# Threshold attention and a squared-ReLU layer on one core: the second visit's turns moved ahead of the first masks, the last chunk's stores given to SyncE's queue

## The chip, the core and the metric

The kernel runs on one core of one Trainium2 chip. The metric is the device time of one execution in microseconds (us). A core has five engines, each working through its own list of instructions in order: TensorE (PE in the profile, with its weight loads as PEld), VectorE (DVE), ScalarE (ACT), GpSimd (POOL) and SyncE (SP), which only issues DMAs and waits. Semaphores order the engines among each other. DMAs are issued here by SyncE's queue, by GpSimd's queue and, at the very start, by ScalarE's.

## The reference

There are 8 batches of 8 heads, each with 576 rows of 64 values. Of each row of scores only those within tau of the maximum keep their weight. The result goes through a two-layer network with a squared ReLU.

```
scores = 0.125 * q @ k^T                                # (8, 8, 576, 576)
scores = where(scores >= max(scores) - tau, scores, -1e9)
attn = exp(scores - max(scores));  attn /= sum(attn) + 1e-9
x = (attn @ v), heads side by side                       # (4608, 512)
out = relu(x @ w_in)**2 @ w_out                          # w_in (512, 2048), w_out (2048, 512)
```

All inputs and the output are float32.

## The kernel before, in words

**Attention.** Heads are taken in pairs, and the work on a pair is cut into visits. The first eight visits split the four head pairs of the first batch in two: visits 0 to 3 take the first two blocks of 128 query rows of each pair, visits 4 to 7 the rest. A visit is a list of steps, one per block of 128 query rows; the first steps are (visit 0, block 0), (visit 0, block 1), (visit 1, block 0), and so on. The rows of a visit's queries and keys lie in `rows_in`, in two sets used alternately; the set for visit 1 lies in a spare part of the tile `wo`, so the profile names it `wo`. Both have to be turned before they can be used: `prep(n)` (L211) calls `prep_part` twice, and each call is one transpose on VectorE (L226), first into `qT`, of which there is one, then into one of two `kT`. The rows themselves were loaded by `load_qk` (L160), whose DMAs are L168 and L171.

**A step** goes through these parts, with the two heads of the pair as two halves of each tile:

- `scores` (L237): matmuls of `qT` with `kT` into the PSUM tiles `s` (L246), and the maxima of each row on VectorE (L268). The tiles of step 1 are called `second`; all others use the same two tiles `s`, so the scores of step 2 must wait for the masks of step 0.
- `exponents` (L278): bias and threshold, then exp, on ScalarE (L281, L282, L284).
- `threshold` (L287): the masks on VectorE (L296), which read scores and exponents, and the sums' reciprocals (L298, L299).
- `divide` (L301): GpSimd scales the weights (L304, L306).
- two steps later `turn` (L321): TensorE turns the weights (L330), ScalarE copies them to `wT` (L331); and `mix` (L429): the products with `v` (L432), which ScalarE copies to `xT`.

**The network.** Once 256 tokens are ready, a chunk of it is queued as pieces (`mlp_in` L473, `product` L540, `pair_in` L635, `mlp_out` L512), and `fill` (L769) puts pieces between the parts of the steps, by the planner's rate. There are 18 chunks (`NCH`). The last two are done together in their first layer. The second layer of a chunk is seven products (L555); what is added up of them in `osb` goes out in two halves of 128 tokens with `store_rows` (L532, the DMA is L534), the second half first. For the last chunk, these are the last things that the program does: a sum on VectorE (L582), a store, one more product, a sum (L585), a store.

**The weights.** They come as 32 pieces by SyncE (L125), and are rounded piece by piece through ScalarE (L138, L139), VectorE (L141, L143) and GpSimd (L145, L147), the first of them at step 2.

**What sets the order.** The schedule is written by hand: what the main loop over steps (L851) emits first comes first on each engine, and the waits follow from which tiles an instruction reads and writes. At the start, ahead of the loop, stand the loads of visits 0 and 1, the values of visit 0, three weight pieces, `prep(0)`, and twenty transposes that only keep TensorE busy (L276). In step 0 the loop emits `scores(0)`, `exponents`, then `scores(1)` at once (L908), then `threshold` and the division. In step 1, which is the last of visit 0, it emits `exponents`, then `prep(1)` (L890, by the flag `lay`), then `threshold`. So VectorE has the order: maxima of steps 0 and 1, masks of step 0, turns for visit 1, masks of step 1, maxima of step 2.

**The end of the program** is line L975: SyncE waits for what is still on its way, every engine drains, and GpSimd collects the others before all end.

Of the kernel before, what the change touches and what calls it, by code (L numbers as in the profile page):

```python
# [19 lines left out]
def kernel(  # L20
# [10 lines left out]
    nc = tc.nc  # L31
# [3 lines left out]
    P = 128  # L35
# [8 lines left out]
    NCH = n_tokens // TCH  # L44
# [52 lines left out]
    osb = const.tile([P, 2, d_model], FP32, name="osb")  # L97
# [62 lines left out]
    def load_qk(n):  # L160


        for x, t in ((rows_of(n)[1], k), (rows_of(n)[0], q)):
            for m in range(4):
                src, to = rows_32(t, n, m), x[m * 32:(m + 1) * 32, :, :]
                queue = nc.scalar if n == 0 and m % 2 else nc.sync
                last = REST // 32 if t is k and m >= 2 and not by_dma(n) else 0
                queue.dma_start(out=to[:, last:, :], in_=src[:, 0:S // 32 - last, :])  # L168
                if last:
                    queue = nc.gpsimd if n == 0 else nc.sync  # L170
                    queue.dma_start(out=to[:, 0:last, :], in_=src[:, S // 32 - last:, :])  # L171
# [39 lines left out]
    def prep(n):  # L211

        prep_part(q, n)
        prep_part(k, n)

    def split_left(n):

        if NBLK in visits[n][1] and not paired(n):
            for u in range(2):
                rows = slice(u * D, (u + 1) * D)  # L220
                nc.scalar.copy(qmid[rows, u * D:(u + 1) * D], qT[rows, NBLK * P:S])

    def prep_part(t, n):
        to, rows = (qT, rows_of(n)[0]) if t is q else (kT[n % 2], rows_of(n)[1])
        arrived(rows)
        nc.vector.transpose(to, rows.rearrange("p c d -> p (c d)"))  # L226
# [10 lines left out]
    def scores(s):  # L237


        vis, i = steps[s]  # L240
        n = 2 if i < NBLK or paired(vis) else 1
        sc = [second[u] if s == 1 else psum.tile([P, 2, 512], FP32, tag=f"s{u}", name=f"s{u}")
              for u in range(n)]

        def term(u, half, rows, lhsT, keys, to=slice(0, P)):
            nc.tensor.matmul(sc[u][to, half, 0:HALF], lhsT, keys[rows, half * HALF:(half + 1) * HALF],  # L246
                             start=True, stop=True)

        if i == NBLK and paired(vis):
            for half in range(2):  # L250
                for v_ in range(2):
                    for u in range(2):
                        rows, cols = slice(u * D, (u + 1) * D), slice(v_ * D, (v_ + 1) * D)
                        term(u, half, rows, qmid[rows, cols], kT[v_], cols)
        elif i == NBLK:
            for half in range(2):
                term(0, half, slice(0, P), qmid, kT[vis % 2])
        else:
            halves = [(half, u) for half in range(2) for u in range(n)]
            if early():  # L260
                halves.sort(key=lambda x: x[1])
            for half, u in halves:
                rows = slice(u * D, (u + 1) * D)
                term(u, half, rows, qT[rows, i * P:(i + 1) * P], kT[vis % 2])
        st = stats[s % len(stats)]
        mx = st[:, 0, 0:n]
        for u in range(n):
            nc.vector.tensor_reduce(out=mx[:, u:u + 1], in_=sc[u][:, :, 0:HALF], axis=AX.XY, op=ALU.max)  # L268

        w = w_slots[(s - first_dma) % (2 if by_dma(vis) else 3)][:, 0:n, :]  # L270
        weights[vis, i] = w, sc, st
# [6 lines left out]
    def exponents(vis, i):  # L278
        w, sc, st = weights[vis, i]
        mx, thr, bias = (st[:, j, 0:len(sc)] for j in range(3))  # L280
        nc.scalar.activation(out=bias, in_=mx, func=AF.Copy, scale=-SCALE)  # L281
        nc.scalar.activation(out=thr, in_=mx, func=AF.Identity, bias=ntau8)  # L282
        for u in range(len(sc)):
            nc.scalar.activation(out=w[:, u, :].rearrange("p (h k) -> p h k", h=2), in_=sc[u][:, :, 0:HALF],  # L284
                                 func=AF.Exp, bias=bias[:, u:u + 1], scale=SCALE)
# [245 lines left out]

    def store_rows(j, t0, t1):  # L532
        lo = j * TCH
        nc.gpsimd.dma_start(out=out[lo + t0 * P:lo + t1 * P, :].rearrange("(t p) d -> p t d", p=P), in_=osb[:, t0:t1, :])  # L534

# [144 lines left out]
    def paired(n):  # L682

        return n >= 3 * HP
# [8 lines left out]
    def by_dma(n):  # L693

        return n >= 3 * HP - 1
# [21 lines left out]
    chunk_at, j = {}, 0  # L717
# [9 lines left out]
    def early():  # L727
        return state["step"] < min(chunk_at)
# [12 lines left out]
    def add_chunk(j):  # L741
        waiting.extend(pieces_of(j))
# [59 lines left out]
    for s, (n, i) in enumerate(steps):  # L802
# [3 lines left out]
        more = nxt < len(visits)  # L806
# [16 lines left out]
        if more:  # L823
            a, b, c, d = (s + 1, s + 5, s + 7, s + 8) if paired(n) else (s + 1, s + 2, s + 4, s + 4)
# [26 lines left out]
    for s in range(END + 1):  # L851
        state["step"] = s
        state["usable"] = rounded_by[-1]
        if s == 2:
            startup.close()
            bpsum = ctx.enter_context(tc.tile_pool(name="bpsum", bufs=1, space=bass.MemoryType.PSUM))
            bank.update((x, bpsum.tile([P, 512], FP32, tag=f"bank{x}", name=f"bank{x}")) for x in range(4, 8))
        rounded_by.append(state["rounded"])
        on = s < NST
        now = []  # L860
        if on:
            n, i = steps[s]
            at = visits[n][1].index(i)
            last = at == len(visits[n][1]) - 1
            now = list(range(done, done + pieces[s]))
            done += pieces[s]
            more = n + 1 < len(visits)
            short = n < 2 * HP
            if short and at == 0 and 0 < n + 1 < 2 * HP:
                load_qk(n + 2)  # L870
            elif not short and at == 1 and not by_dma(n):
                load_qk(n + 1)
            if now:
                round_weights(now[0], 0)
            if s != 1:
                scores(s)
        old = steps[s - 2] if 2 <= s < NST + 2 and not by_dma(steps[s - 2][0]) else None
        at_once = now or old or early()
        lay = on and last and more and not by_dma(n)
        if old:  # L880
            turn(*old, 0)
            turn(*old, 1)
        if on:
            exponents(n, i)
            for p in now[1:]:
                round_weights(p, 0)
            if at == 1:
                split_left(n)
            if lay:
                prep(n + 1)  # L890
            elif now:
                for p in now:
                    round_weights(p, 1)
        if s in mixes and not old:
            mix(*mixes[s])
            for j in chunk_at.get(s, ()):
                add_chunk(j)
        quarter = rate(s) / 4 if s < END else 1e9
        fill(quarter)
        if s in mixes and old:  # L900
            mix(*mixes[s])
            for j in chunk_at.get(s, ()):
                add_chunk(j)
        if old:
            turn(*old, 2)
        state["free"] = s > first_dma
        if s == 0:
            scores(1)  # L908
        if on:
            threshold(n, i)  # L910
            for fn in prep_at[s] + load_at[s]:
                fn()
            if lay and now:
                round_weights(now[0], 1)
            if now:
                round_weights(now[0], 2)
                round_weights(now[0], 3)
            for p in now[1:]:
                assert not lay
                round_weights(p, 2)  # L920
                round_weights(p, 3)
            if not at_once:
                divide(n, i)
        if 0 < s <= NST and by_dma(steps[s - 1][0]):
            m, x = steps[s - 1]
            turn_blocks(m, x)
        for what in place_at[s]:
            place_blocks(*what)
        some_loads()
        fill(quarter)  # L930
        some_loads()
        if on and at_once:
            divide(n, i)
        fill(quarter)
        some_loads()
        fill(quarter)
        some_loads()
        if on:
            for p in now:
                end_rounding(p)  # L940
            if at == 0 and 0 < n <= 2 * HP:
                load_v(n)
            elif last and n >= 2 * HP and not by_dma(n):
                load_v(n + 1)
# [35 lines left out]
```

## Time and profile before

The times of four runs were 1382.0, 1383.06, 1383.14 and 1384.55 us.

| What | us |
|---|---|
| median of the four runs | 1383.1 |
| the profiled execution | 1383.01 |
| its span in the profile | 1380.9 |
| TensorE busy (share of the span) | 1345.7 (97%) |
| GpSimd busy | 882.0 (64%) |
| VectorE busy | 874.5 (63%) |
| ScalarE busy | 432.9 (31%) |

The span runs from the first instruction of the program to the last one; 2.1 us of the profiled execution's time lie outside it. An engine counts as busy while one of its instructions runs. A row of a timeline gives start, duration, engine, line and operation, and in brackets how long the engine had stood idle before it and what ended that. A DMA's row shows its issue alone; when its data has landed is a separate figure. The granted clock of TensorE is the share of full speed that its clock gate allowed in a stretch of time.

### The profile page before, as it was taken

To read this page: it belongs to the slowest core of one execution; us is meant where nothing else is said; L and a number is where in the kernel's file an instruction comes from. 1 tells how busy PE (TensorE), PEld (TensorE's weight loads), DVE (VectorE), ACT (ScalarE), POOL (GpSimd) and SP (SyncE) were. 2 spreads that over 40 slices of the span, in tenths; PEclk is the share of its full clock that TensorE was granted. 3 is DMA by queue.
4 is the path that set the end of the run, shared out by engine and by line. 5 is a ranking of instruction groups with operands and counts; after the bars stand their busy time and mean duration, and the time that the engine had idled before them with its cause. 6 is when DMAs were issued, how large, how long until landed. Compare 5 with 4: busy or idle time off the path is not lost.

```text
span 1380.9 us, 22711 instructions
## 1 busy us (share of the span) xinstructions
PE 1345.7 (97%) x7544; PEld 1032.9 (75%) x7544; DVE 874.5 (63%) x1974; ACT 432.9 (31%) x1060; POOL 882.0 (64%) x1195
## 2 busy tenths in 40 slices
PE   6898999999999999999999999999999999999998
PEld 4676556777777777777777777777777777788887
DVE  5877675967767676757575666566666666432641
ACT  4776674223232323232322222222222222200000
POOL 3678875668786868676767768585868665423031
PEclk8999999999999999999999999999999999999999
DMA  8764541445645455554445455544545644320000
GB/s 153 160 154 110 143 93 27 88 85 106 118 94 116 98 106 118 104 113 84 97 85 114 85 111 109 107 76 100 91 101 98 122 82 95 62 52 0 16 0 31
DMA packets 407747, 127.94 MB, mean 93 GB/s; under 512 B 390832, under 2 KB 396752, under 8 KB 407632
## 3 DMA queue, kind: packets, MB, share of 16 engines
q1 hardware_dynamic: 385344, 94.57, 36.6%
q0 software_dynamic: 19984, 31.63, 8.6%
q8 instruction: 61, 1.00, 0.3%
q10 hardware_dynamic: 2304, 0.29, 0.2%
q14 instruction: 54, 0.44, 0.1%
HBM read 50.59 MB, written 9.44 MB: 43 GB/s over the span
## 4 chain that ended last, share of the span: by engine, by line
PE 89%; DVE 3%; ACT 3%; POOL 2%; issue 1%; DMA 0%; POOLq 0%; SPq 0%; DVEq 0%; ACTq 0%
PE bank L480 31%; PE bank L555 29%; PE s L246 12%; PE bank L432 11%; PE bank L653 2%; PE bank L521 2%; PE bank L330 2%; PE pair L653 1%; ACT wT L331 1%; ACT w L284 1%; DVE st L268 1%; DVE wo L509 1%; DVE w L296 1%; POOL g L493 0%; POOL w L306 0%
## 5 line engine op out<-in xcount | busy, mean ns | idle before, releaser
L480 PE MATMUL bank<-xT,w_in_sb 128*128 128x256 f32 x2048 | 464.8, 383 | 3.1 <-POOL w_in_sb L147 2.1
L480 PEld LDWEIGHTS bank<-xT,w_in_sb 128*128 128x128 f32 x2048 | 382.4, 190 | 78.9 <-issue 21.7
L268 DVE TENSOR_REDUCE st<-s 128x1 f32<-128x576 f32 x286 | 204.0, 752 | 221.1 <-PE s L246 220.9
L296 DVE SCALAR_TENSOR_TENSOR w<-s,st,w 128x576 f32<-128x576 f32 x269 | 209.2, 815 | 120.6 <-ACT w L284 120.5
L306 POOL TENSOR_SCALAR w<-w,st 128x576 f32<-128x576 f32 x269 | 222.7, 837 | 25.4 <-DVE st L299 19.6
L555 PE MATMUL bank<-wo,gsum 128*128 128x256 f32 x1024 | 234.6, 382 | 2.3 <-POOL gsum L470 2.3
L555 PEld LDWEIGHTS bank<-wo,gsum 128*128 128x128 f32 x1024 | 191.9, 190 | 39.6 <-issue 9.8
L281 ACT ACTIVATE st<-st 128x2 f32<-128x2 f32 (+1 forms) x148 | 30.3, 205 | 564.8 <-DVE st L268 564.1
L284 ACT ACTIVATE w<-s,st 128x576 f32<-128x576 f32 x269 | 183.1, 731 | 0.2 <-ACT st L282 0.2
L370 DVE STREAM_TRANSPOSE turned<-w 128x512 f32<-128x512 f32 (+2 forms) x388 | 168.9, 490 | 21.4 <-DMA wT<-turned 19.5
L246 PE MATMUL s<-kT,qT 64*128 64x288 f32 x1016 | 165.6, 433 | 12.4 <-DVE kT L226 5.2
L555 PE MATMUL bank<-wo,g 128*128 128x256 f32 x768 | 177.5, 382 | 0.0
L493 POOL TENSOR_TENSOR g<-g 128x512 f32<-128x512 f32 x128 | 135.7, 1061 | 62.3 <-ACT g L492 61.0
L304 POOL TENSOR_SCALAR st<-st 128x2 f32<-128x2 f32 (+1 forms) x148 | 32.7, 221 | 220.9 <-DVE w L296 213.7
L432 PE MATMUL bank<-wT,vs 128*64 128x128 f32 (+7 forms) x1700 | 168.1, 356 | 5.0 <-ACT wT L331 3.4
L555 PEld LDWEIGHTS bank<-wo,g 128*128 128x128 f32 x768 | 143.9, 190 | 28.6 <-issue 8.7
L432 PEld LDWEIGHTS bank<-wT,vs 128*64 128x64 f32 (+1 forms) x1700 | 95.7, 137 | 76.9 <-issue 24.8
L246 PEld LDWEIGHTS s<-kT,qT 64*128 64x128 f32 x1016 | 94.3, 188 | 68.7 <-issue 49.0
L492 ACT ACTIVATE g<-bank 128x512 f32<-128x512 f32 x128 | 76.5, 600 | 114.3 <-PE bank L480 113.7
L190 POOL DMA_DIRECT2D vs<-in_v_dram x144 | 90.5, 633 | 0.0
L470 POOL TENSOR_TENSOR gsum<-g 128x512 f32<-128x512 f32 x32 | 41.4, 1293 | 48.0 <-DVE g L668 45.7
L145 POOL TENSOR_TENSOR turned<-turned 128x512 f32<-128x512 f32 x32 | 41.0, 1285 | 40.9 <-DVE turned L143 35.0
(130 smaller groups left out, 1186.9 us busy)
## 6 DMA issues: line engine op xcount, KB each, us to landing
wT<-turned SPq DMA_DIRECT2D x800, 72.0 KB, 2.3
out_dram<-osb POOLq DMA_DIRECT2D x34, 256.0 KB, 2.9
wo<-in_moe_w_in_dram SPq DMA_DIRECT2D x16, 512.0 KB, 4.7
wo<-in_moe_w_out_dram SPq DMA_DIRECT2D x16, 512.0 KB, 3.7
ql<-in_q_dram POOLq DMA_DIRECT2D x96, 72.0 KB, 2.7
wT<-turned SPq DMA_DIRECT2D x192, 36.0 KB, 2.3
kl<-in_k_dram POOLq DMA_DIRECT2D x88, 72.0 KB, 3.1
vs<-in_v_dram POOLq DMA_DIRECT2D x48, 128.0 KB, 3.1
```

The source lines that it names most:

```text
L190: (nc.gpsimd if state["step"] > first_dma + 2 else nc.sync).dma_start(out=to, in_=src)
L246: nc.tensor.matmul(sc[u][to, half, 0:HALF], lhsT, keys[rows, half * HALF:(half + 1) * HALF], start=True, stop=True)
L268: nc.vector.tensor_reduce(out=mx[:, u:u + 1], in_=sc[u][:, :, 0:HALF], axis=AX.XY, op=ALU.max)
L284: nc.scalar.activation(out=w[:, u, :].rearrange("p (h k) -> p h k", h=2), in_=sc[u][:, :, 0:HALF], func=AF.Exp, bias=bias[:, u:u + 1], sca ...
L296: nc.vector.scalar_tensor_tensor(out=wu, in0=sc[u][:, :, 0:HALF], scalar=thr[:, u:u + 1], in1=wu, op0=ALU.is_ge, op1=ALU.mult, accum_out=s ...
L306: nc.gpsimd.tensor_scalar(out=w[:, u, :], in0=w[:, u, :], scalar1=z[:, u:u + 1], scalar2=rcp[:, u:u + 1], op0=ALU.add, op1=ALU.mult)
L370: nc.vector.transpose(wb[:, at:at + k1 - k0, i % 2, :], w[:, u, k0 * 32:k1 * 32].rearrange("p (k q) -> p k q", q=32))
L432: nc.tensor.matmul(ps[u * D:(u + 1) * D, :], vs[n % 2][rows, u * (NBLK + 1) + c, :], wT[rows, NBLK if c == NBLK else u * (NBLK + 1) + c, a ...
L480: nc.tensor.matmul(h[:, x % 2, :], w_in_sb[:, c, f * P:(f + 1) * P], xT[:, c, at:at + TCH], start=(c == 0), stop=(c == NMC - 1))
L492: nc.scalar.activation(out=to, in_=h, func=AF.Relu)
L493: nc.gpsimd.tensor_tensor(out=to, in0=to, in1=to, op=ALU.mult)
L555: nc.tensor.matmul(to, left[:, f, :], wo[:, slot, f, :], start=(f == 0), stop=(f == HF - 1))
```

## The change

There are two edits. The first emits `prep(1)` in step 0, right behind `scores(1)`, and takes it out of step 1. On VectorE the two transposes then stand behind the maxima of steps 0 and 1 and ahead of the masks of step 0. The second issues the two stores of the last chunk from SyncE's queue instead of GpSimd's; all other chunks' stores stay on GpSimd's.

```diff
     def store_rows(j, t0, t1):
         lo = j * TCH
-        nc.gpsimd.dma_start(out=out[lo + t0 * P:lo + t1 * P, :].rearrange("(t p) d -> p t d", p=P), in_=osb[:, t0:t1, :])
+        (nc.sync if j == NCH - 1 else nc.gpsimd).dma_start(out=out[lo + t0 * P:lo + t1 * P, :].rearrange("(t p) d -> p t d", p=P), in_=osb[:, t0:t1, :])
...
-        lay = on and last and more and not by_dma(n)
+        lay = on and last and more and not by_dma(n) and s != 1
...
         if s == 0:
             scores(1)
+            prep(1)
         if on:
             threshold(n, i)
```

## The prediction

> **What bounds the kernel now.** I read the page first. In its chain that ended last TensorE holds nine tenths, and part 1 has it busy for 1345.7 of 1380.9 us.
>
> ```profile
> PE 89%; DVE 3%; ACT 3%; POOL 2%; issue 1%; DMA 0%; POOLq 0%; SPq 0%; DVEq 0%; ACTq 0%
> ```
>
> The change touches no matmul, so it can only act where TensorE is not the bound: in the first 30 us and after the last matmul. I therefore asked for the timelines of VectorE and TensorE over the start. VectorE's columns are start, duration, engine, line:
>
> ```profile
> 11.19 1.41 DVE L268 TENSOR_REDUCE st<-second 128x1 f32<-128x576 f32 x2
> 12.52 0.81 DVE L296 SCALAR_TENSOR_TENSOR w<-s,st,w 128x576 f32<-128x576 f32 x1
> ...
> 13.25 0.81 DVE L296 SCALAR_TENSOR_TENSOR w<-s,st,w 128x576 f32<-128x576 f32 x1
> ...
> 14.55 0.78 DVE L226 STREAM_TRANSPOSE qT<-wo 128x576 f32<-128x576 f32 x1
> 15.25 0.74 DVE L226 STREAM_TRANSPOSE kT<-wo 128x576 f32<-128x576 f32 x1
> 15.91 0.78 DVE L296 SCALAR_TENSOR_TENSOR wo<-second,st,wo 128x576 f32<-128x576 f32 x1
> ...
> 18.43 1.42 DVE L268 TENSOR_REDUCE st<-s 128x1 f32<-128x576 f32 x2 [0.53 <-PE s L246]
> ```
>
> VectorE runs without a break from 9.85 to 17.9 us: maxima, masks of step 0, turns of the second visit's rows, masks of step 1. Only before the maxima of step 2 does it stand idle, for 0.53 us, and it waits for TensorE's scores.
>
> ```profile
> 9.65 1.24 PE L246 MATMUL second<-kT,qT 64*128 64x288 f32 x8
> 16.13 2.30 PE L246 MATMUL s<-kT,qT 64*128 64x288 f32 x8 [5.24 <-DVE kT L226]
> 18.36 2.18 PE L330 MATMUL bank<-ident,w 128*128 128x128 f32 x9
> 22.34 2.99 PE L246 MATMUL s<-kT,qT 64*128 64x288 f32 x8 [1.80 <-DVE w L296]
> ```
>
> TensorE stands idle 5.24 us until the turned keys are there, then needs 2.30 us for eight matmuls that took 1.24 us just before. The stretches of the granted clock (the column after POOL's) say why:
>
> ```profile
> 14.00:15.00 1.00, 0.00 (x0) 0.00 (x0) 0.85 (x5) 0.49 (x1) 0.51 (x2) 1.00 0.89 188
> 15.00:16.00 1.00, 0.00 (x0) 0.00 (x0) 1.00 (x3) 0.00 (x0) 1.00 (x2) 0.58 0.87 242
> 28.00:29.00 1.00, 1.00 (x12) 0.57 (x8) 0.71 (x1) 0.89 (x2) 0.38 (x1) 0.59 0.92 172
> 29.00:30.00 1.00, 1.00 (x9) 0.70 (x7) 0.96 (x5) 0.61 (x2) 0.05 (x1) 1.00 1.03 209
> ```
>
> The clock falls to half at 15.17 us and comes back at 28.82 us: 13.65 us at half clock (the trace's own clock events have these two times). In between the chain of waits runs scores, turns (L330), copies (L331), exponents, masks, and scores again, so TensorE's halved rate is in it.
>
> The end, in three views: the last row of the timeline, what SyncE's queue waited for, and the instructions of the closing line L975 (durations in ns, then first and last start):
>
> ```profile
> 1376.21 0.54 POOL L534 DMA_DIRECT2D out_dram<-osb  x1 [2.65 <-DVE osb L585]
> ```
> ```profile
> SPq L975 <- DMA out_dram<-osb: 153.4, 1, 153.4
> ```
> ```profile
> L975 POOLq EVENT_SEMAPHORE  x4: 17/17/17, 1380.1 to 1380.8; - x4
> L975 POOLq DRAIN  x3: 46/98/3912, 1376.2 to 1380.6; - x3
> L975 SPq DRAIN  x3: 7/7/13, 1379.0 to 1380.4; - x3
> ```
>
> The last sum is ready at 1375.48 + 0.43 = 1375.91 us. GpSimd issues the store 0.30 us later; it lands 2.32 us on, at 1378.53 (landing 2.3 in all answers on L534 at the end). SyncE, which had waited 153 us for nothing else, is through its own drain by 1379.1. But GpSimd's drain, begun at 1376.2 with the store still to be issued, takes 3.91 us and ends at 1380.1; its next step, collecting the other engines, comes only then, and 0.74 us later the span is over. So **the end hangs on GpSimd's drain, 1.0 us after SyncE was done**.
>
> **The Trainium skill.** "TensorE: Matmul & The Clock Gate", Part 1, says that the clock is set over free-running windows of about 3.4 us, that an idle window halves it and a busy one restores it. The trace agrees: 13.65 us are four such windows, and the window that ended at 15.17 had no matmul in it. How much work saves a window the page does not say; here 0 is too little, 0.5 of a window enough (the clock stayed up through the half-filled window that ended at 1377.1). "DMA: Bandwidth & Descriptors", Latency and other measured facts, gives a first byte after some 0.6 us from SyncE's queue and 1 us from GpSimd's; in the packets of the trace it is 0.96 to 0.98 us (undisturbed weight loads of L125) and 1.11 us (the last stores). "Perfetto Trace Analysis", DMA Instruction — SWDGE (GPSIMD), says that such a record ends with the making of the descriptors; 0.54 us recorded against 2.32 us to landing agrees. No page tells of a drain behind a store.
>
> **Part A, the turns moved ahead.** Nothing is added: the same two L226 instructions, 0.70 and 0.66 us from start to start, or 1.36 us, go before the masks of step 0 instead of behind them. They issue no DMA and pass no queue but VectorE's. Behind them now stand the masks of step 0, and for those wait GpSimd (L304, L306) and TensorE's next use of the score tiles.
> Do the turns wait? Their rows were issued by SyncE from 3.9 to 8.9 us; the last landed at 8.44 + 2.51 = 10.95 us, 1.6 us before 12.52. TensorE's last reading of the old qT was over at 10.9. So no wait, and the turns run from 12.52 to 13.9. The masks of step 0 start at 13.88 and 14.61 and the divisions follow; the sum up to step 1's masks is the same, so those stay at 15.91 and VectorE is free for the maxima of step 2 at 17.73 + 0.18 = 17.91.
> TensorE: at step 3 the trace shows how scores follow masks at half clock. First mask at 21.37, scores from 22.34 (0.97 later); second mask at 22.11, scores done at 25.34 (3.23 later). So scores of step 2 run from 13.88 + 0.97 = 14.85 to 14.61 + 3.23 = 17.84, against 16.13 to 18.43: **0.59 us earlier**. The maxima gain 18.43 - 17.91 = 0.52 us of the same. What is late next: the turns of step 0 (L330) need its division, which GpSimd now ends 1.36 us later, at 16.33 + 1.36 = 17.69; that is just before the scores end, so it costs nothing while the clock is low. At full clock it and VectorE's 17.91 would be the bound, and the cover is gone. The copies (L331, the second at 19.94) and ScalarE's L281 at 20.32 come 0.59 us earlier, since ScalarE has finished the weights' L138 and L139 at 18.4. From there on the order is unchanged and every step waits on the one before; the third visit's rows have landed at 23.9 against 26.05 for their turns, so no DMA eats the shift. The dense stage after it is a fixed order of work, so I carry it to the end in full: **-0.6 us**. Both ends: 0, if TensorE had been at full clock (scores would have ended by 17.4, behind VectorE's 17.9 anyway); and the gain of the clock itself. Its price: from the scores of step 2 to those of step 4, 16.13 to 29.55, are 13.42 us at half clock; two later steps at full clock, 34.52 to 45.34, take 10.82. So 2.6 us, the 0.6 included. Between them: a clock that comes back one window sooner, 3.41 us at half rate saved, about half of it: -0.6 - 1.2 or so. TensorE's gap shrinks from 5.24 us to 14.85 - 10.90 = 3.95, still longer than a window of 3.41, and 0.3 us of matmuls at its end is little. I take that the clock still falls in most runs.
>
> **Part B, the last two stores.** GpSimd loses two issues (0.56 and 0.54 us), SyncE's queue gets two. The queue it goes to is empty: SyncE has waited since 1225 us. SyncE starts a DMA 0.03 us after VectorE's end where that was the release (a load behind L226), so the issue is at about 1375.95, not 1376.21. No row shows a 256 KB store from SyncE. Lower bound: the 72 KB moves of L382 land in 2.3 (2.1 at least); upper: the 512 KB loads of L125 in quiet stretches, 3.4. I take 2.35, since GpSimd's own store of this size takes 2.32 and its first byte 1.11. Landing: 1378.3. SyncE's closing waits and drain took 0.56 us from landing (1378.53 to 1379.09), GpSimd's collecting some 0.06, the rest 0.74: the span ends at 1379.66 instead of 1380.88. GpSimd's drain starts after L580 (1369.87) and is then long over. **-1.2 us**; ends -1.5 (2.1 to landing) and -0.2 (3.4). The first of the two stores lands 3 us earlier and sets nothing.
>
> **Sum.** The profiled execution took 1383.0 us, with 2.1 us outside its span, 0.1 below the median of 1383.1: 1383.0 - 0.6 - 1.2 = **1381.2 us**.
>
> **Rivals.** (1) The clock stays up: with matmuls from 14.85 on, the window that ended at 15.17 is no longer empty. For it: the one empty window is what halved the clock. Against: 0.3 of 3.4 us, and where the windows lie may differ from run to run. 1383.0 - 2.6 - 1.2 = 1379.2 us. (2) Part A is hidden, since VectorE's 17.9 or the division at 17.7 bounds step 2: 1383.0 - 1.2 = 1381.8. For it: VectorE has only 0.53 us of idle time to give. (3) Slower: the turns wait for their rows at 12.52 and hold the masks of step 0 behind them, a wait that was harmless at 14.55. Place: the first L226 at 12.5 us. Price: a microsecond for each beyond 10.95 + 1.6. The longest landing of L168 in the first 30 us is 6.3 us, of loads beside the weights; that would put the rows at 8.44 + 6.3 = 14.7, the scores 2.2 us later, at 20.0 against 18.43. With part B: 1383.0 + 1.6 - 1.2 = 1383.4. It decides from landings over 2.51 + 1.6 + 0.6 + 1.2 = 5.9 us. Against it: the eight loads all landed within 2.5 to 3.7 us.
>
> **How the numbers follow.** Forecast 0.47, clock stays up 0.28, hidden 0.20, slower 0.05. Some 0.2% (2.8 us) is what a measurement of this kernel can tell from no change. Faster by more needs under 1380.3: all of rival 1, and of the forecast the part in which the clock recovers a window sooner (0.04): 0.32. Slower by more: the far end of rival 3, 0.03. Within: 0.65. Range: from a little under rival 1, 1379.0, to 1382.6, which is rival 2 with the store nearly at its slow bound (1383.0 - 0.4).
>
> **What would show it.** In the profile after: the L226 pair at 12.5 with no wait; scores of step 2 from 14.85; the maxima of step 2 at 17.9; the clock's fall and return (none at all: rival 1); L281 of step 2 at 19.7. At the end: a store on SyncE's queue at about 1376 minus the shift, landing 2.35 us later, and GpSimd's first collecting step within 0.7 us of it. A landing over 3.4 us, or a GpSimd drain that ends late all the same, makes part B wrong; a shift at the first dense matmuls that is not found at the last makes the carrying wrong.

## The result and the profile after

The changed kernel takes 1380.26 us (median of 31 runs, 1379.2 to 1381.84) against 1383.09 us of the kernel before (49 runs, 1381.71 to 1384.71). The ratio is 0.998 with an interval from 0.9975 to 0.9985: **2.83 us less**, where 1.8 had been forecast. The profiled execution took 1380.32 us with a span of 1378.5; 1.8 us lie outside it, against 2.1 before.

VectorE's timeline at the start:

```profile
12.62 0.77 DVE L226 STREAM_TRANSPOSE qT<-wo 128x576 f32<-128x576 f32 x1
13.31 0.73 DVE L226 STREAM_TRANSPOSE kT<-wo 128x576 f32<-128x576 f32 x1
13.97 0.78 DVE L296 SCALAR_TENSOR_TENSOR w<-s,st,w 128x576 f32<-128x576 f32 x1
...
15.87 0.80 DVE L296 SCALAR_TENSOR_TENSOR wo<-second,st,wo 128x576 f32<-128x576 f32 x1
...
17.79 1.40 DVE L268 TENSOR_REDUCE st<-s 128x1 f32<-128x576 f32 x2
```

The turns start right behind the maxima and wait for nothing (no bracket). Step 1's masks start within 0.04 us of where they did (15.87 against 15.91), and the 0.53 us of idle time ahead of the maxima of step 2 are gone. In this execution everything up to the turns is 0.10 us late, because the first rows landed 0.10 us later, so 17.79 stands for 17.69. TensorE's timeline:

```profile
14.90 2.99 PE L246 MATMUL s<-kT,qT 64*128 64x288 f32 x8 [3.91 <-DVE w L296]
17.83 2.18 PE L330 MATMUL bank<-ident,w 128*128 128x128 f32 x9
21.81 3.00 PE L246 MATMUL s<-kT,qT 64*128 64x288 f32 x8 [1.80 <-DVE w L296]
```

It now waits for masks where it waited for the turned keys, 3.91 instead of 5.24 us, and the two groups of eight that take 2.99 and 3.00 us run at half clock, as the stretches show (length of the stretch, busy time of PE, PEld, DVE, ACT and POOL, then the granted clock):

```profile
14.00:15.00 1.00, 0.10 (x1) 0.13 (x1) 1.00 (x4) 0.59 (x1) 0.00 (x0) 0.96 0.79 205
15.00:16.00 1.00, 1.00 (x4) 0.85 (x6) 0.86 (x5) 0.00 (x0) 0.23 (x1) 0.50 0.84 209
28.00:29.00 1.00, 1.00 (x9) 0.60 (x7) 1.00 (x3) 0.53 (x2) 0.00 (x0) 0.72 1.25 171
```

The clock still falls, at 14.91 us, for 13.65 us. Every instruction of VectorE and ScalarE can be set against its counterpart before: from 21 us on nearly all are 0.50 to 0.54 us earlier, still 0.52 at the last chunk. With the late start added, part A is worth 0.62 us.

The end, by the closing line (now L976) and what SyncE's queue waited for:

```profile
L976 POOLq EVENT_SEMAPHORE  x4: 17/17/17, 1377.8 to 1378.4; - x4
L976 POOLq DRAIN  x3: 46/98/3712, 1368.6 to 1378.2; - x3
L976 SPq DRAIN  x3: 7/7/7, 1377.7 to 1378.0; - x3
```

```profile
SPq L534 <- DVE osb L582: 154.5, 1, 154.5
SPq L534 <- DVE osb L585: 3.0, 1, 3.0
SPq L976 <- DMA out_dram<-osb: 1.3, 1, 1.3
```

GpSimd's long drain, 3.71 us, is over at 1372.3, before the last sum. It collects the others at 1377.8, right behind SyncE's drain at 1377.7. The last sum is ready at 1375.39; from there to the end of the span are 3.1 us, where it was 5.0.

### The profile page after: what moved, and what is told of

Its sections match the earlier page's. It is cut to its first block, busy times and chain, and to the rows that moved or that the text cites. A ratio compares the mean times of both kernels' runs of the same rounds, so it can differ in the third digit from the quotient of the medians.

```text
span 1378.5 us, 22712 instructions
## 1 busy us (share of the span) xinstructions
PE 1346.4 (98%) x7544; PEld 1033.4 (75%) x7544; DVE 874.7 (63%) x1974; ACT 432.9 (31%) x1060; POOL 880.8 (64%) x1193
## 4 chain that ended last, share of the span: by engine, by line
PE 90%; DVE 3%; ACT 3%; POOL 2%; issue 1%; DMA 0%; ACTq 0%; DVEq 0%; POOLq 0%
PE bank L480 31%; PE bank L555 29%; PE s L246 12%; PE bank L432 11%; PE bank L653 2%; PE bank L521 2%; PE bank L330 2%; PE pair L653 1%; ACT wT L331 1%; ACT w L284 1%; DVE st L268 1%; DVE wo L509 1%; DVE w L296 1%; POOL g L493 0%; POOL w L306 0%
## 5 line engine op out<-in xcount | busy, mean ns | idle before, releaser
L281 ACT ACTIVATE st<-st 128x2 f32<-128x2 f32 (+1 forms) x148 | 30.3, 205 | 565.2 <-DVE st L268 564.5
```

## Experiments

A finding about the times themselves comes first. The runs of each kernel lie in three groups. Before: around 1382.1 (12 of 49), 1383.1 (31) and 1384.6 us (6); after: around 1379.5 (7 of 31), 1380.25 (18) and 1381.7 (6). All three moved; their shares hardly did. The profiles tie the groups to where the clock rises and falls. In the middle group (before, after, part A alone) there is one stretch of 13.65 us at half clock; in the lower group (part B alone, the small copy and the cut store below) the clock is up for 3.4 us in the middle of it; the one profile of the upper group is shown further down. One to three profiles for each group make this likely, not certain. All edits below are against the changed kernel. The kernel before ran along with each set, with medians of 1383.09 to 1383.21 us, so the changed kernel's 1380.26 serves as the mark for all.

**Each part alone.** First part A:

```diff
-        (nc.sync if j == NCH - 1 else nc.gpsimd).dma_start(...)
+        nc.gpsimd.dma_start(...)
```

> Part A alone, the stores back on GpSimd's queue. Theory: part A is a constant shift of 0.5 to 0.6 us that the dense stage carries to the end, so 0.6 us under the kernel before, and the end of the program is as it was (GpSimd's drain ends 1.0 us after SyncE's). Rival: the two parts are not independent, and the last sum comes no earlier, or the whole gain of 2.8 us is the start's: 0 or 2.8 us.

Measured: 1382.52 us (13 runs) against 1383.21 on the same chip. The ratio, 1.0001 (0.9992 to 1.0009), can't tell 0.7 us from nothing; that part A gains rests on the trace. There masks and scores of step 2 are where they are in the changed kernel, to 0.01 us, and the last sum is 0.57 us earlier than before in spite of a start that is 0.10 us late: 0.67 us. The difference of the medians, 0.69 us, is of that size. 2.15 us lie outside the profiled span, as before.

Part B alone:

```diff
-        lay = on and last and more and not by_dma(n) and s != 1
+        lay = on and last and more and not by_dma(n)
...
             scores(1)
-            prep(1)
```

> Part B alone, the turns back in step 1. Theory: 1.9 us in the span (the drain of GpSimd is off the end, the store lands in 2.1 us) and 0.3 us of the time outside the span, so 2.2 us under the kernel before. Rival: the 0.3 us outside the span belongs to the start, or the store's queue is worth only the 1.2 us predicted: 1.2 to 1.9 us.

Measured: 1381.05 us (21 runs) against 1383.21, 2.16 less, ratio 0.9987 (0.998 to 0.9993); 1.8 us outside the span. In the medians 0.69 and 2.16 make 2.85, so the parts add up as far as these can tell; the interval of this ratio alone runs from 1.0 to 2.8 us. The 0.3 us outside the span belong to the stores.

**What holds the end.** A small GpSimd instruction behind the last sum, with no DMA on GpSimd's queue:

```diff
-                return [lambda: store_rows(j, 0, 1)]
+                def end():
+                    store_rows(j, 0, 1)
+                    if j == NCH - 1:
+                        nc.gpsimd.tensor_copy(out=p5s[:, 0:1], in_=osb[:, 0, HD:HD + 1])
+                return [end]
```

> The changed kernel with one small copy of 128 x 1 on GpSimd that waits for the last sum; its result is not used, and no DMA is on GpSimd's queue at the end. Theory: GpSimd's drain takes some 3 us behind its last instruction of any kind, so it ends at about 1378.6 us instead of long before SyncE's 1377.7, and 0.8 to 1.0 us of part B are lost in the span. Rival: the drain waits for DMAs that GpSimd issued; there is none here, and the time is that of the changed kernel to 0.2 us.

Measured: 1381.33 us (13 runs), 1.07 above the changed kernel; the ratio to the kernel before is 0.9988 (0.9979 to 0.9996). The closing line of this kernel, from its profile:

```profile
L980 POOLq EVENT_SEMAPHORE  x4: 17/17/17, 1377.7 to 1378.3; - x4
L980 POOLq DRAIN  x3: 46/97/3143, 1374.5 to 1378.1; - x3
L980 SPq DRAIN  x3: 7/7/13, 1376.6 to 1377.9; - x3
```

The copy took 0.18 us and ended at 1374.66; the drain ended at 1374.46 + 3.14 = 1377.6, 2.95 us behind it, and GpSimd collected only then, 1.0 us after SyncE was through. From the last sum to the end of the span are 4.06 us, against 3.12 in the changed kernel. So the drain needs no DMA to be long: it ended 2.95 us behind a sum (after), 2.95 behind a copy, 3.34 behind the issue of a store (before). The rival, a drain that is long only for DMAs that GpSimd issued, is out.

Only the very last store on SyncE's queue:

```diff
-        (nc.sync if j == NCH - 1 else nc.gpsimd).dma_start(...)
+        (nc.sync if j == NCH - 1 and t0 == 0 else nc.gpsimd).dma_start(...)
```

> The changed kernel with only the very last of the two stores on SyncE's queue, the one before it back on GpSimd's. Theory: GpSimd's drain then starts 3.2 us earlier than in the kernel before and ends at about 1376.4 us, ahead of SyncE's, so nothing is lost in the span; the 0.3 us outside the span come back only if they belong to a store of GpSimd near the end: 0.0 to 0.3 us over the changed kernel. Rival: any store by GpSimd near the end holds the end: 1 us or more over it.

Measured: 1380.42 us (14 runs), ratio 0.9981 (0.9973 to 0.9989), within 0.2 us of the changed kernel, with 1.8 us outside the span. GpSimd's drain of 3.85 us began at 1373.9 and was over at 1377.8, SyncE's came at 1379.3. Of part B the second store alone would have done.

**The clock.** Four kernels put transposes of the identity into TensorE's gap. The first two:

```diff
+    def keep_clock(times):
+        for x in range(times):
+            nc.tensor.transpose(second[1][:, x % 2, HALF:HALF + P], ident, ident)
...
             scores(1)
             prep(1)
+            keep_clock(34)
```

> The changed kernel with 34 transposes of the identity into unused columns of step 1's score tile, right behind step 1's scores, so that TensorE is busy in its gap of 3.9 us. They compute nothing that is used. Theory: the clock no longer falls to half at 14.9 us, scores of step 2 take 1.9 us from first to last instead of 3.0, and the time is 2.0 us under the changed kernel (4.8 under the one before). Rival: the stage is bound by VectorE, ScalarE and GpSimd, and the clock hardly matters: 0.0 to 0.5 us under the changed kernel.

> The same 34 transposes, with part B but without part A. Theory: at full clock the scores of step 2 end by 17.4 us, before VectorE is free at 17.9, so part A is hidden there, and this is the same as with part A to 0.2 us: 4.6 to 4.8 us under the kernel before. Rival: part A's shift is worth its 0.6 us at any clock: 4.2 us under the kernel before.

Measured: 1380.78 us (21 runs, ratio 0.9985, 0.9979 to 0.9992) and without part A 1380.98 (21 runs, 0.9986, 0.998 to 0.9993). Neither came near the 2 us of the theories; the two differ by 0.2 us, as the second theory had it, but the test was not the one I meant. ScalarE's timeline of the first (its lines have moved: L289 is the exp, L281 the added transposes):

```profile
14.49 0.72 ACT L289 ACTIVATE wo<-second,st 128x576 f32<-128x576 f32 x1
18.18 0.74 ACT L289 ACTIVATE wo<-second,st 128x576 f32<-128x576 f32 x1 [2.97 <-PE second L281]
```

The transposes waited for the maxima of step 1 and held its second exponent back 2.97 us, though they use columns that nobody else does. A second pair, with 24 transposes ahead of the first scores, others (30, or 42 without part A) in columns beyond all that is read, and 20 more behind the turns of step 0:

```diff
-    keep_busy(20)
+    keep_busy(24)
...
             scores(1)
             prep(1)
+            keep_clock(second[1], 30)
...
             turn(*old, 2)
+        if s == 2:
+            keep_clock(weights[n, i][1][1], 20)
```

> The changed kernel with TensorE kept busy through the start: 24 instead of 20 transposes of the identity ahead of the first scores, 30 into columns of step 1's score tile that nobody reads, right behind step 1's scores, and 20 into such columns of step 2's tile, behind the turns of step 0. None computes anything that is used, and unlike the 34 tried before they wait for no maxima. Theory: the clock stays up from 10 us on, the scores of step 4 start at about 27 us instead of 29.2, and the median is 2 us under the changed kernel, some 4.8 under the one before. Rival: what bounds these steps is the chain of VectorE and ScalarE, and 1.0 us or less is gained.

> The same without part A (and 42 instead of 30 transposes, since the gap is longer). Theory: at full clock VectorE, free at 17.9 us either way, bounds the maxima of step 2, part A is hidden, and this is equal to the run with part A to 0.2 us. Rival: the shift of part A is worth its 0.5 to 0.6 us at full clock too, and this is that much slower than the run with part A.

Measured: 1382.41 us (13 runs, 0.9993, 0.9985 to 1.0002) and 1383.62 (13 runs, 1.0001, 0.9993 to 1.0009). In the first, transposes waited for the maxima of step 1 (1.8 us) and for step 2's exponent (2.4 us), and held up step 1's second exponent (2.3 us) and the masks of step 2 (3.6 us), so it is no test either. In the profile of the second the clock did not fall at all, and still the scores of step 4 started only at 30.51 us, against 29.55 before the change. It differs in the number of transposes too. **Whether part A would be hidden at full clock is left open.**

What these profiles do show is that a window of the clock need not be empty for a fall. The ends of the windows follow from the clock's own events, in steps of 3.41 us; the second number behind a stretch is TensorE's busy time in it. From the kernel with 34 transposes and without part A, and from part B alone:

```profile
13.96:17.38 3.42, 3.42 (x32) 3.09 (x30) 2.58 (x8) 0.76 (x2) 1.86 (x3) 1.00 0.86 287
17.38:20.79 3.41, 1.55 (x13) 0.96 (x9) 3.23 (x7) 2.70 (x7) 1.85 (x3) 1.00 1.03 255
20.79:24.20 3.41, 2.15 (x7) 1.89 (x8) 2.21 (x7) 1.26 (x3) 0.62 (x1) 0.50 0.82 132
```

```profile
20.91:24.32 3.41, 1.94 (x9) 1.36 (x10) 2.77 (x8) 1.47 (x3) 0.41 (x1) 1.00 0.80 127
24.32:27.73 3.41, 3.41 (x25) 2.75 (x26) 2.61 (x5) 2.39 (x6) 3.24 (x5) 0.50 0.58 94
```

Windows with 1.55 and 1.94 of 3.41 us of matmuls, 45% and 57%, still ended in a fall. Rival 1 counted on some 0.3 us of step 2's scores at the end of a window. In the changed kernel's profile the window ended at 14.91, with 0.01 us of them. The kernel with 24 transposes ahead of the first scores, told of below, has both parts too, and in its profile the window ended later, behind 0.68 us of these very matmuls. The clock fell all the same:

```profile
12.07:15.49 3.42, 0.68 (x3) 0.60 (x4) 3.33 (x7) 2.42 (x6) 0.00 (x0) 1.00 0.60 146
15.49:18.90 3.41, 3.41 (x13) 2.36 (x12) 3.22 (x10) 1.46 (x3) 2.90 (x6) 0.50 1.00 364
```

A test that nobody waits for: nine transposes into a bank that step 2 does not use, behind the turns of step 0.

```diff
             turn(*old, 2)
+        if s == 2:
+            for x in range(9):
+                nc.tensor.transpose(bank[6][:, 0:P], ident, ident)
```

> The changed kernel with nine transposes of the identity into a PSUM bank that nobody uses in step 2, behind the turns of step 0, so that TensorE is busy from 17.8 us until the scores of step 3 without anyone waiting for them. They compute nothing that is used. Theory: halved clock is a cost in these steps; with a busy window behind 17.8 us it comes back between 21 and 24.7 us instead of 27 to 28.6, and the median falls by 0.8 to 1.1 us, to the group of executions that lie there already. Rival: the chain of VectorE and ScalarE bounds these steps and the clock is worth nothing, or the nine hold up the scores of step 3: 0 to 0.5 us slower.

Measured: 1378.58 us (6 runs), ratio 0.9969 (0.9958 to 0.998), 1.7 us under the changed kernel. TensorE's timeline (L908 are the nine) and a stretch of its profile:

```profile
17.76 2.18 PE L330 MATMUL bank<-ident,w 128*128 128x128 f32 x9
19.73 1.89 PE L908 MATMUL bank<-ident 128*128 128x128 f32 x9
21.74 1.94 PE L246 MATMUL s<-kT,qT 64*128 64x288 f32 x8
...
27.00 1.94 PE L246 MATMUL s<-kT,qT 64*128 64x288 f32 x8 [0.64 <-DVE w L296]
```

```profile
21.00:22.00 1.00, 0.88 (x6) 0.68 (x5) 1.00 (x3) 0.74 (x2) 0.00 (x0) 0.88 0.85 139
```

With no idle time from 14.8 to 26.4 us, the clock is back at 21.24 us for good; the scores of step 3 take 1.94 instead of 3.00 us and those of step 4 start at 27.00 instead of 29.16. Of these 2.16 us, 1.73 are left at step 5 and 1.61 at the last sum. The theory had the size too low: it stopped at the group of executions that lay lower already, and there the clock had fallen once more (in part B alone: up at 20.9, down at 24.3, up at 27.7).

24 instead of 20 transposes ahead of the first scores, alone:

```diff
-    keep_busy(20)
+    keep_busy(24)
```

> The changed kernel with 24 instead of 20 transposes of the identity ahead of the first scores, so that TensorE has no gap of 0.9 us there. Theory: the executions some 1.5 us above the median are those in which the clock came up only at 12.5 us, behind the first scores; with the gap filled the clock is up by 10.1 us in all, that group goes, and the median stays or falls by up to 0.3 us. Rival: that group has another cause, and stays at about one in five.

Measured: 1380.12 us (13 runs), ratio 0.9978 (0.997 to 0.9987); none of 13 lies above 1380.32. At one in five, the share in the changed kernel, none of 13 would come about one time in 18; at the 6 in 49 of the kernel before, about one time in five. So this speaks for the theory without settling it. The profile of the kernel with only the last store on SyncE's queue is one of the upper group (1381.86 us), and in its timeline the first scores take 2.30 us, where they took 1.25 before: its clock came up at 12.45 us only, by the clock's events:

```profile
8.52 2.30 PE L246 MATMUL s<-kT,qT 64*128 64x288 f32 x8 [0.76 <-DVE ntau L847]
```

**The last store cut in two.**

```diff
+    def store_part(t, cols):
+        lo = (NCH - 1) * TCH + t * P
+        nc.sync.dma_start(out=out[lo:lo + P, cols], in_=osb[:, t, cols])
...
                 tt(out=osb[:, 0, 0:HD], in0=to, in1=p1s, op=add)
+                if j == NCH - 1:
+                    return [lambda: store_part(0, slice(0, HD))]
...
+                if j == NCH - 1:
+                    return [lambda: store_part(0, slice(HD, d_model))]
                 return [lambda: store_rows(j, 0, 1)]
```

> The changed kernel with the very last store cut in two by columns: the half whose sum (L577) has long been ready goes out behind that sum, and only the other 128 KB wait for the last sum. Theory: the end is the last store's way to memory, of which some 0.8 us are its packets; half of them gone gives 0.4 us under the changed kernel. Rival: the first packet and the confirmation, 0.9 and 0.4 us, are all that counts, and nothing is gained.

Measured: 1379.76 us (9 runs), ratio 0.9975 (0.9965 to 0.9984), 0.5 us under the changed kernel; its last 128 KB landed 1.70 us after their issue, where 256 KB took 2.06.

The nine transposes, the 24 and the cut store together, on the changed kernel:

> The last three edits together. Theory: they add up, at 1.2 to 1.5 us under the changed kernel and some 4.2 under the one before. Rival: with the clock up early the nine transposes and the 24 undo each other's gain, and only the split store's 0.4 us are left.

Measured: **1378.08 us** (5 runs, 1378.0 to 1378.22), ratio 0.9964 (0.9952 to 0.9977): 2.2 us under the changed kernel and 5.0 under the one before, more than the 1.2 to 1.5 expected; alone the three had brought 1.7, 0.1 and 0.5 us. The five runs lie within 0.22 us; that the groups have gone rests on these five.

## Why the prediction came out as it did

Both parts went the way that was written, and their sum was too small, by the end of the program. The measured 1380.26 us lies just under the 1380.3 below which the prediction looked for the clock's gains alone; it was the end of the program that took it there, not the clock. Point by point:

- **The turns do not wait, the order on VectorE holds.** Right: with this execution's late start of 0.10 us taken off, the first masks are 1.35 us later (1.36 forecast) and the scores of step 2 start at 14.80 (14.85 forecast); step 1's masks moved by little, and the maxima of step 2 have no idle time ahead.
- **Part A, -0.6 us, carried to the end.** Right: 0.62 us in the trace of both parts, 0.67 in that of part A alone, and none of it lost on the way. The runs' times alone would not have shown it.
- **Part B, -1.2 us.** The mechanism was right, the size was not: 2.16 us. Three terms of the sum were mis-sized. The landing was put at 2.35 us behind the issue, by GpSimd's own 2.32; it took 2.06. SyncE's closing waits were put at 0.56 us behind the landing; they took 0.26, since the queue had gone through six of the nine while the store was under way (their rows stand between 1375.8 and 1376.2), where before the second of them held the queue up for 153 us and seven came behind it. And 0.3 us more came from outside the span, of which the prediction had nothing; the runs tie it to a last store that GpSimd does not issue, and not to the drain (with the small GpSimd copy it stayed away); why is open. In the span: 1.22 + 0.29 + 0.30 + 0.04 for the issue and the collecting = 1.85; from the last sum to the end there were 4.97 us before and 3.12 after, which is 1.85 as well.
- **GpSimd's drain.** That it held the end is shown by the small copy. The picture behind it, a drain behind a store, was too narrow: it ended some 3 us behind a sum and a copy too.
- **Rival 1, the clock stays up.** Wrong: the clock fell in every profile of a kernel with both parts or one and no added matmuls, and behind 0.68 us of step 2's scores too. The reading that a half-filled window is enough, taken from the one that ended at 1377.1, does not hold either: windows with 52% (the small copy, up to 23.54 us) and 57% ended in a fall. The price of rival 1, 2.0 us for the clock alone, was somewhat high: with the nine transposes the scores of step 4 come 2.16 us sooner, but 1.6 to 1.7 us reach the end.
- **Rival 2, hidden.** Wrong at the clock that these runs had; at full clock it is open. **Rival 3, waiting rows.** No wait in the profile of the changed kernel.

## What to carry to other kernels

Read the last microseconds of a program by itself: find which engine's closing step is late, and let the engine with the long drain do its last instruction some 4 us before the end (2.95 us of drain and 0.74 us of closing here, by the traces). The time that part A saved in the start-up chain came through the whole dense stage undiminished; the order behind it is fixed and no DMA bound it, though that this is the reason was not tested. And fill an idle stretch of TensorE in such a chain only with work that no other engine's tile depends on: nine such matmuls paid 1.7 us, while 34 in a shared tile brought nothing or cost 0.5 us.

## What the runs showed of the hardware

- GpSimd's drain ended 2.95 to 2.96 us behind a sum or a copy and 3.27 to 3.34 us behind the issue of a store.
- A 256 KB store landed 2.04 to 2.10 us after its issue from SyncE's queue and 2.28 to 2.32 from GpSimd's; 128 KB from SyncE's 1.69 to 1.80.
- A window of the clock needed no emptiness for a fall, and the share of matmuls alone did not decide: with 45%, 52% and 57% it fell, while with 44% (after, the window that ended at 1376.83) and 52% (before, the one that ended at 1377.1) it stayed. What decides is left open; the window with 57% held the scores' matmuls, of the form 64*128, the two at the end those of 128*128. The Trainium skill, "TensorE: Matmul & The Clock Gate", Part 1, has the clock fall after an idle window; here it fell after windows that were not idle as well.
- Matmuls waited for readers of other columns of the same PSUM tile (1.8 and 2.4 us), and readers for them (2.3 to 3.6 us).
